# A planner's urgency table, two issuing queues for w_out, and four more weight pieces split on TensorE

## The chip, the cores and the metric

The kernel runs on one core of one Trainium2 chip. The time is device microseconds of that core; lower is better. The kernel before was timed three times: 793.66, 795.12 and 795.73 us, median 795.12.

## The reference, cut to what matters

Block-sparse attention over 4 batches, 8 heads, 768 positions of 64, in blocks of 32 positions; its output is the input of a two-matrix network with the activation h * tanh(softplus(h)).

```python
scores = scale * np.matmul(q, k.transpose(0, 1, 3, 2))
mask = np.abs(blk_i - blk_j) <= 1          # window
mask |= first or last block, as query or as key
for qb in range(n_blocks):                 # and three sampled blocks for each query block
    for kb in sampled_blocks[qb]: mask[...] = True
attn = softmax(where(mask, scores, -1e9)); x = attn @ v      # (3072, 512) after the heads are joined
h = x @ w_in                               # 512 -> 2048
g = h * np.tanh(softplus(h))
out = g @ w_out                            # 2048 -> 512
```

w_in and w_out come as 64-bit floats of 8 MB each; the kernel decodes them itself.

## The kernel before

Every fp32 operand is split into a high and a low fp16 part, so a product is three fp16 matmuls. The work is made of tasks, each with one engine (or a choice of engines), a planned duration, its dependencies and a number `key`. `Plan.emit` writes the instructions of all engines in one pass: for each engine it takes the task that can start first by the planned durations, and among tasks that can start within 0.02 us of each other the one with the smallest ready time plus `key`. The result is a fixed order of instructions on each engine. The engines run these orders in sequence and wait for each other through semaphores.

The work has three kinds.

- **Attention** has 52 jobs, 13 for each batch. A job is one dense query block (the first or the last) or a pair of sparse ones. Its chain runs: scores `s` (L634, PE), maximum `mx` (L681, DVE), exponential `pt` (L700, ACT), transposes `t` (L640, PE), high part `ph` (L723, ACT), low part `pl` (DVE L727; in the first six jobs a matmul with `neg`, L731, and an ACT copy, L736), the product with v into `obank` (L762, PE), a scaling `xs` (L784, DVE), a transpose `tx` (L640), and high and low parts `xh`, `xl` (L809, L818). `xh` and `xl` are rings of three tiles of 256 positions. Tile 0 is complete when job 4 has written its `xl`. From job `WHOLE` on, the keys of a query block are gathered into one piece, so that its scores take half as many matmuls. From job `SPLIT` on, both halves of the product with v are one task.
- **Weights.** w_in comes in 8 pieces of 1 MB (`wr`), w_out in 16 of 0.5 MB (`wor`), issued by ACT (L838). `wor` uses the ring `raw` of six buffers, which holds q, k and v as well. DVE decodes each with three instructions (L846, L849, L852). A bf16 product on PE (`gram`, L334) gives each its scale. A half piece of w_in is then split either on PE (`wd_i`: a matmul with a scaled diagonal, L918, and one with `neg`, L927, with casts on ACT or DVE), or with `wt_i` on ACT, DVE and POOL. `LPE` says how many of four go to PE. w_out is split with `wt_o` (L934 to L941), after all 16 of its pieces have been decoded, since they share one scale (`tp_wo`).
- **MLP.** 12 tiles; `h` (L1016) has 16 tasks of 12 matmuls for a tile, `y` (L1075) 16 tasks of 6. Both keep their order.

MLP tasks have the lowest rank on PE: they go where nothing else can start. Scores are held back by `START` (a planned time for each of the first 14 jobs; a held task still runs when nothing else is ready) and after that by `RES` (L1227, L1242): a job's scores come late until the MLP work done has reached its even share of the total less `RES`. The total is 12 tiles of 16 tasks of 1.31 us and 16 of 1.30 us, or 501 us.

Between 14 and 200 us of planned time, gaps of PE are filled with matmuls that nobody reads (`fill`, L1264), one for each 0.14 us.

Of the kernel before, what the change touches and what calls it, by code (L numbers as in the profile page):

```python
# [29 lines left out]

class Task:
# [9 lines left out]
class Plan:  # L41
# [141 lines left out]
def attn_mish_kernel(ctx: ExitStack, tc: tile.TileContext, qT, kT, v, sampled, blocks, w_in, w_out, out):  # L183
# [117 lines left out]
    NO, NZ = 4 * (D + 2), 240  # L301
    pools = {"w": ctx.enter_context(tc.tile_pool(name="never", bufs=1))}
# [317 lines left out]
    WHOLE = 14  # L620
    SPLIT = 12
# [20 lines left out]
    def attend(job):  # L642
# [188 lines left out]
    def load_w(pool, key, tag, w, a0):  # L831

        if not wide:
            nc.scalar.dma_start(out=a0, in_=w)
# [3 lines left out]
        nc.scalar.dma_start(out=raw.rearrange("p (c f) -> p c f", c=w.shape[1]) if len(w.shape) == 3 else raw, in_=w)  # L838
        tl[key] = raw.rearrange("p (f two) -> p f two", two=2)
# [21 lines left out]
    def load_i(k):  # L861
# [143 lines left out]
    def moe_h(st, fp):  # L1005
        b, t = st
        kh, kq = ("h", b, t, fp), ("hs", b, t, fp // 2)

        def fn(f2):
# [5 lines left out]
            for k, (w, x, cc) in enumerate(prods):  # L1015
                nc.tensor.matmul(h[:, f2].rearrange("p (s q) -> p s q", q=BS), wi[:, fp, cc // 2, w, cc % 2, fs], x[:, :, cc],  # L1016
                                 start=f2 == 0 and k == 0, stop=f2 == 1 and k == len(prods) - 1)
        for f2 in range(2):
            mlp(1.31, lambda f2=f2: fn(f2), r=[*PARTS_I(fp), *xt["x", b, t]], w=[kh, "h in order"],
                new=[("h", kh)] if f2 == 0 else (), use=[("xh", b, t), ("xl", b, t)])  # L1020

        def hs_fn():
            if fp % 2 == 0:
                new(sb, "hs", kq, [P, 4, TT])
            nc.scalar.activation(out=tl[kq][:, 2 * (fp % 2):2 * (fp % 2) + 2], in_=tl[kh], func=AF.Copy,  # L1025
                                 scale=gsc[:, fp:fp + 1])
        add("ACT", 0.72, hs_fn, r=[kh, "gsc"], w=[("hsw", b, t, fp)],
            new=[("hs", kq)] if fp % 2 == 0 else (), use=[kq], key=-4)
        if fp % 2 == 1:
            moe_g(st, fp // 2)  # L1030

    def moe_g(st, k):

        b, t = st
        kq, ku, kg = ("hs", b, t, k), ("us", b, t, k), ("g", b, t, k)
        us, hs, g = (lambda: tl[ku]), (lambda: tl[kq]), (lambda: tl[kg])

        def u_fn():
# [274 lines left out]
```

## Time and profile before

| | |
|---|---|
| time, median of three runs | 795.12 us |
| the profiled execution: time, and its span | 799.4 us, 797.6 us |
| mean granted clock of TensorE | 0.984 |
| PE busy | 747.6 us (94%) |
| ACT, DVE, POOL busy | 542.9, 490.4, 324.2 us |
| moved by DMA | 95.33 MB |

A row of the profile names a line, an engine, an operation, what is written and what is read. "Busy" is the time in which at least one instruction of the group runs. An idle time is put down to whatever ended it. PE is TensorE's matmuls, PEld its weight loads, DVE VectorE, ACT ScalarE, POOL GpSimd and SP SyncE; ACTq and SPq are the instructions that issue DMAs. The span begins with the first instruction and ends with the last; the profiled execution's time is 1.8 us longer than its span.

### The profile page before, as it was taken

To read this page: it belongs to the slowest core of one execution; us is meant where nothing else is said; L and a number is where in the kernel's file an instruction comes from. 1 tells how busy PE (TensorE), PEld (TensorE's weight loads), DVE (VectorE), ACT (ScalarE), POOL (GpSimd) and SP (SyncE) were. 2 spreads that over 40 slices of the span, in tenths; PEclk is the share of its full clock that TensorE was granted. 3 is DMA by queue.
4 is the path that set the end of the run, shared out by engine and by line. 5 is a ranking of instruction groups with operands and counts; after the bars stand their busy time and mean duration, and the time that the engine had idled before them with its cause. 6 is when DMAs were issued, how large, how long until landed. Compare 5 with 4: busy or idle time off the path is not lost.

```text
span 797.6 us, 30868 instructions
## 1 busy us (share of the span) xinstructions
PE 747.6 (94%) x12901; PEld 527.8 (66%) x12901; DVE 490.4 (61%) x897; ACT 542.9 (68%) x881; POOL 324.2 (41%) x397
## 2 busy tenths in 40 slices
PE   6778889798999999999999999999999999999997
PEld 5654668576667777676677766766767767666653
DVE  6868867997776756657746665675676544323220
ACT  3555667769876877787757777878675766465650
POOL 2032246896643544535424543436444231312031
PEclk9999989999999999999999999999999999999999
DMA  8988874304344355246223553343344313000000
GB/s 305 288 242 270 234 193 134 93 21 144 93 143 123 96 162 179 72 110 196 67 82 98 157 154 103 104 150 92 98 125 117 106 40 92 14 14 14 14 14 26
DMA packets 57743, 95.33 MB, mean 120 GB/s; under 512 B 8323, under 2 KB 20612, under 8 KB 57604
## 3 DMA queue, kind: packets, MB, share of 16 engines
q1 hardware_dynamic: 50880, 76.32, 32.6%
q10 hardware_dynamic: 6724, 17.05, 6.7%
q8 instruction: 101, 1.65, 0.9%
q14 instruction: 38, 0.31, 0.1%
HBM read 80.38 MB, written 12.95 MB: 117 GB/s over the span
## 4 chain that ended last, share of the span: by engine, by line
PE 77%; DMA 8%; DVE 7%; ACT 3%; issue 2%; SPq 2%; POOL 1%; POOLq 1%; ACTq 0%; DVEq 0%
PE y L1075 29%; PE h L1016 27%; PE obank L762 6%; PE t L640 6%; PE s L634 5%; DMA wor<-in_moe_w_out_dram 2%; DMA raw_q<-in_q_dram 2%; DMA wr<-in_moe_w_in_dram 2%; DVE wt_o L936 1%; PE tx L640 1%; PE obank L1264 1%; PE wd_i L918 1%; SPq L595 1%; DVE us L1043 1%; DMA raw_k<-in_k_dram 1%
## 5 line engine op out<-in xcount | busy, mean ns | idle before, releaser
L1016 PE MATMUL h<-xh,wi 128*128 128x256 f16 x1536 | 283.5, 274 | 0.0
L1075 PE MATMUL y<-wo,g 128*128 128x512 f16 x1152 | 279.4, 381 | 1.5 <-POOL g L1060 1.5
L1016 PEld LDWEIGHTS <-wi 128*128 128x128 f16 x2304 | 223.0, 98 | 47.3 <-issue 3.0
L1016 PE MATMUL h<-xl,wi 128*128 128x256 f16 x768 | 210.0, 273 | 0.0
L1060 POOL TENSOR_TENSOR g<-hs,g 128x1024 f16<-128x1024 f32 x48 | 109.2, 2276 | 203.7 <-DVE g L1057 137.6
L1075 PEld LDWEIGHTS <-g 128*128 128x128 f16 x1152 | 110.6, 99 | 103.0 <-issue 3.4
L571 POOL COPY kg<-kt 128x256 f16 x255 | 107.8, 454 | 154.3 <-PE s L634 137.3
L1025 ACT ACTIVATE hs<-h,gsc 128x512 f32<-128x512 f32 x96 | 65.5, 684 | 83.0 <-PE h L1016 82.6
L700 ACT ACTIVATE pt<-s,nb,ns 128x256 f32<-128x256 f32 (+1 forms) x208 | 107.2, 580 | 7.5 <-DMA wor<-in_moe_w_out_dram 2.6
L727 DVE SCALAR_TENSOR_TENSOR pl<-t,ph 128x512 f16<-128x512 f32 x99 | 68.0, 687 | 63.4 <-ACT ph L723 63.2
L723 ACT ACTIVATE ph<-t 128x512 f16<-128x512 f32 x112 | 66.7, 596 | 52.7 <-PE t L640 50.0
L1049 DVE SCALAR_TENSOR_TENSOR hs<-us,hs 128x1024 f32<-128x1024 f32 x48 | 60.9, 1268 | 43.6 <-ACT us L1048 43.6
L681 DVE TENSOR_REDUCE mx<-s 128x4 f32<-128x1024 f32 x44 | 53.8, 1222 | 45.5 <-PE s L634 45.5
L1045 POOL TENSOR_TENSOR us<-us 128x1024 f32<-128x1024 f32 x26 | 51.9, 1997 | 60.7 <-DVE us L1043 57.6
L640 PE MATMUL t<-ident,pt 128*128 128x128 f32 x448 | 70.6, 281 | 4.8 <-DVE pl L727 4.4
L640 PEld LDWEIGHTS t<-ident,pt 128*128 128x128 f32 x448 | 53.2, 143 | 18.8 <-DVE pl L727 5.2
L762 PEld LDWEIGHTS <-ph 128*32 128x32 f16 x3584 | 48.0, 94 | 21.7 <-issue 11.8
L1039 ACT ACTIVATE us<-hs,hsc 128x1024 f32<-128x1024 f32 x48 | 55.2, 1151 | 1.2 <-DVE hs L1049 0.5
L1047 ACT ACTIVATE us<-us 128x1024 f32<-128x1024 f32 x48 | 50.7, 1056 | 5.5 <-POOL us L1045 4.7
L762 PE MATMUL obank<-vg,ph 128*32 128x65 f16 (+1 forms) x3200 | 50.7, 196 | 2.1 <-DMA vg<-vd 1.1
L1043 DVE TENSOR_SCALAR us<-us 128x1024 f32<-128x1024 f32 x48 | 39.2, 818 | 19.4 <-ACT us L1039 19.3
L1048 ACT ACTIVATE us<-us 128x1024 f32<-128x1024 f32 x48 | 50.7, 1056 | 0.7
(204 smaller groups left out, 920.8 us busy)
## 6 DMA issues: line engine op xcount, KB each, us to landing
vg<-vd SPq DMA_DIRECT2D x320, 65.0 KB, 2.4
vg<-vd SPq DMA_DIRECT2D x80, 195.0 KB, 3.0
wr<-in_moe_w_in_dram ACTq DMA_DIRECT2D x8, 1024.0 KB, 7.0
wor<-in_moe_w_out_dram ACTq DMA_DIRECT2D x16, 512.0 KB, 6.4
vd<-v SPq DMA_DIRECT2D x12, 520.0 KB, 3.9
vg<-vd SPq DMA_DIRECT2D x12, 520.0 KB, 3.8
raw_k<-in_k_dram SPq DMA_DIRECT2D x12, 512.0 KB, 5.0
raw_q<-in_q_dram SPq DMA_DIRECT2D x12, 512.0 KB, 4.4
```

The lines of the kernel that those rows point to most:

```text
L571: nc.gpsimd.tensor_copy(out=dst, in_=tl["kt", b][:, :, ds(j, BS)])
L640: nc.tensor.matmul(out, src, ident, start=start, stop=stop, is_transpose=True)
L700: ex = lambda o, x, g, w: nc.scalar.activation(out=o, in_=x, func=AF.Exp, bias=nb[:, g, w:w + 1], scale=tl["ns", b, sus[w]["qb"] // TB][:, ...
L723: nc.scalar.activation(out=new(sb, "ph", ("ph", i, j), [P, 2, 2, P], F16), in_=tl["t", i, j], func=AF.Copy, scale=PSC)
L727: nc.vector.scalar_tensor_tensor(out=new(sb, "pl", ("pl", i, j), [P, 2, 2, P], F16), in0=tl["t", i, j], scalar=PSC, in1=tl["ph", i, j], op ...
L762: nc.tensor.matmul(o[cs, w, g, 0:v1 - v0], p[:, k, g, cs], vt[:, k, 2 * c + g, v0:v1], start=j == 0 and g == 0 and k == 0 and n == 0, stop ...
L1016: nc.tensor.matmul(h[:, f2].rearrange("p (s q) -> p s q", q=BS), wi[:, fp, cc // 2, w, cc % 2, fs], x[:, :, cc], start=f2 == 0 and k == 0, ...
L1025: nc.scalar.activation(out=tl[kq][:, 2 * (fp % 2):2 * (fp % 2) + 2], in_=tl[kh], func=AF.Copy, scale=gsc[:, fp:fp + 1])
L1039: nc.scalar.activation(out=new(sb, "us", ku, [P, 4, TT]), in_=hs(), func=AF.Exp, scale=hsc[:, b:b + 1])
L1049: add("DVE", 1.32, lambda: nc.vector.scalar_tensor_tensor(out=hs(), in0=us(), scalar=-0.5, in1=hs(), op0=ALU.add, op1=ALU.mult), r=[ku], w ...
L1060: add("POOL", 2.3, lambda: nc.gpsimd.tensor_tensor(out=g()[:, 1], in0=hs(), in1=g()[:, 0], op=ALU.subtract), r=[kq, ("gh", b, t, k)], w=[kg])
L1075: nc.tensor.matmul(tl[ky], tl["g", b, t, k][:, g, f, q], wo[:, fc, w], start=fc == 0 and n == 0, stop=fc == NFC - 1 and n == 2)
```

## The change

A table adds a number to the key of each task: by its kind, for attention in the first 14 jobs also by the job, and for weights also by the piece. A load of a weight may be issued by ACT or by SP, and the planner chooses. The rest are numbers, and code for half tiles that does not run, because `NHV` is 0 and `HALVES` is empty: `part` is always None.

```diff
+URGE = {"am": -2, "dgi": -11, "endsv": 10, "gh": 6, "gp": -24, "gram": 15, ..., "xw": -3, "ys": -3}
+JOBS = [-11, -1, -1, -13, 3, 4, 2, -13, -38, 3, -19, -28, -1, -34]
+PIECES = [0, 2, -3, -3, -1, -1, 2, 2, -20, -23, -13, -9, -8, -8, -8, -8, -6, -1, -1, 1, -1, 3, 6, 6]
...
+        kind_, i, k = place(w)
+        key += URGE.get(kind_, 0.0) + (JOBS[i] if i is not None else 0.0) + (PIECES[k] if k is not None else 0.0)
...
-    WHOLE = 14
-    SPLIT = 12
+    WHOLE = 12
+    SPLIT = 10
...
+            go = lambda eng: load_w(pools["w"], raw, "wr", src, None, eng)
+            add("ACT", 0.45, lambda: go(nc.scalar), r=after, w=[raw], new=[("wr", raw)], key=-9, lat=2.0,
+                kind=("dma", 3.9), also=[("SP", 0.5, lambda: go(nc.sync), False)] if BOTH else ())
...
+        add("ACT", 0.45, lambda: go(nc.scalar), r=after, w=[raw] + ([] if wide else [("wo", fc)]), new=[("raw", raw)],
+            key=-5, lat=2.0, kind=("dma", 1.95), also=[("SP", 0.5, lambda: go(nc.sync), False)] if BOTH else ())
...
-    LPE = 3
+    LPE = 4
-    AT0, ATV, ATW = -19.0, -13.0, 1.0
+    AT0, ATV, ATW = -19.0, -13.0, -4.0
+    NHV = 0
...
-            PREP = (6, 4, 3) if b else (8, 4, 7)
+            PREP = (6, 4, 3) if b else (7, 3, 6)
-            LOADO, ATO, ATP = [("dec", 5)], -2.0, -22.0
+            LOADO, ATO, ATP = [("dec", 6)], -2.0, -22.0
...
-    RES, START = 145.0, [0, 72, 75, 102, 72, 15, 93, 69, 30, 51, 33, 45, 51, 66]
+    RES, START = 510.0, [0, 99, 19, 112, 114, 119, 80, 0, 11, 132, 80, 43, 18, 0]
```

`PREP` says how many jobs before the end of a batch the next batch's k, v and q are loaded; `LOADO` after which decoded piece of w_in the loads of w_out may begin. A tile of `xl` is still complete when the same jobs have written it.

What this does to the orders is seen at three places. First, on ACT, at the first loads of w_out. Before:

```order
L809 ACTIVATE xh_0_1293<-tx_1653 128x256
L700 ACTIVATE pt_1676<-s_1395,nb_1673,ns_0_270 128x256 x2
L838 DMA wor_1707<-in_moe_w_out_dram 128x1024
L838 DMA wor_1715<-in_moe_w_out_dram 128x1024
L838 DMA wor_1735<-in_moe_w_out_dram 128x1024
L838 DMA wor_1739<-in_moe_w_out_dram 128x1024
L838 DMA wor_1755<-in_moe_w_out_dram 128x1024
L818 ACTIVATE xl_0_1294<-tx_1653 128x256
L723 ACTIVATE ph_0_1768<-t_0_1709 128x512
```

And of the change, at its first loads on ACT:

```order
L951 ACTIVATE wi<-wd_i_0_1998 128x512
L865 DMA wor_2093<-in_moe_w_out_dram 128x1024
L750 ACTIVATE ph_0_2099<-t_0_2039 128x512
L865 DMA wor_2121<-in_moe_w_out_dram 128x1024
L865 DMA wor_2123<-in_moe_w_out_dram 128x1024
L951 ACTIVATE wi<-wd_i_0_2101 128x512
L865 DMA wor_2129<-in_moe_w_out_dram 128x1024
L763 ACTIVATE pl_0_2230<-t_0_2039 128x512
```

Five loads in a row have become four with work between them, and they stand later. ACT issues 8 of the 16 loads, where it issued all.

Second, on SP, which gathers blocks of v (`vg`) for the sparse jobs; the other 8 loads of w_out now stand between the gathers. Before:

```order
L595 DMA vg_112<-vd_60 32x1040
L392 DMA raw_q_2_2331<-in_q_dram 128x4x256
L588 DMA vg_113<-vd_60 96x1040
L595 ISA
L595 DMA vg_113<-vd_60 32x1040
```

Of the change:

```order
L622 DMA vg_112<-vd_60 32x1040
L865 DMA wor_2235<-in_moe_w_out_dram 128x1024
L865 DMA wor_2242<-in_moe_w_out_dram 128x1024
L419 DMA raw_q_2_2325<-in_q_dram 128x4x256
L615 DMA vg_113<-vd_60 96x1040
L622 ISA
L622 DMA vg_113<-vd_60 32x1040
```

Two loads have come ahead of q and of the next gather; two more pairs and two single loads follow at later gathers. The loads of w_in all stay on ACT.

Third, on PE, at job 4's last matmuls on `tx`, after which tile 0 lacks only `xl`. Before:

```order
L815 MATMUL tx_2964<-xh_0_1293,neg 128x128
L815 LDWEIGHTS neg
L815 MATMUL tx_2964<-xh_1_2979,neg 128x128
L918 MATMUL wd_i_0_3039<-wi,dg_i_2967 128x512
L634 LDWEIGHTS q_1_1656
L634 MATMUL s_3060<-kt_228,q_1_1656 32x96
```

Of the change:

```order
L842 MATMUL tx_2943<-xh_1_3090,neg 128x128
L758 LDWEIGHTS neg
L758 MATMUL t_0_2908<-ph_0_3053,neg 128x512
L956 LDWEIGHTS neg
L956 MATMUL wd_i_1_3050<-wi,neg 128x512
L1309 LDWEIGHTS neg
L1309 MATMUL obank<-neg 128x240
```

From the last row on `tx` to the first `h` it was 522 rows on PE, with the scores of two jobs and three pieces of `wd_i`; it is now 115 rows: the two matmuls with `neg`, six fill matmuls, four transposes and one product with v (48 matmuls).

Counted over the whole order of PE, fill matmuls go from 171 to 102: those ahead of the first `h` from 146 to 102, those behind it from 25 to none. The split pieces `wd_i` go from 12 to 16, all ahead of the first `h`. Score matmuls with 96 and 160 columns of keys go down by 48 each, those with 256 up by 48. Ahead of the first `h` now stand the scores of 7 jobs instead of 8, with 96 fewer matmuls, 48 fewer products with v, one fewer each of `t` and `tx` and 8 fewer of w_out's gram.

Behind it, 3 `h` and 3 `y` tasks stood between the scores of one job and of the next for most of the program; now it is 2 and 2 in most places, with stretches of 10 and 10 now and then. At the last job's scores both orders have 149 `h` and 133 `y` tasks, of 192 each, behind them.

More of the change, by code (lines that the diff above doesn't have):

```diff
@@ L1024, in hs_fn @@
                 new(sb, "hs", kq, [P, 4, TT])
-            nc.scalar.activation(out=tl[kq][:, 2 * (fp % 2):2 * (fp % 2) + 2], in_=tl[kh], func=AF.Copy,
+            nc.scalar.activation(out=tl[kq][:, 2 * (fp % 2):2 * (fp % 2) + 2, 0:n], in_=tl[kh][:, :, 0:n], func=AF.Copy,
                                  scale=gsc[:, fp:fp + 1])
-        add("ACT", 0.72, hs_fn, r=[kh, "gsc"], w=[("hsw", b, t, fp)],
+        add("ACT", 0.72 if part is None else 0.45, hs_fn, r=[kh, "gsc"], w=[("hsw", b, t, fp, part)],
@@ L1038, in u_fn @@
         def u_fn():
-            nc.scalar.activation(out=new(sb, "us", ku, [P, 4, TT]), in_=hs(), func=AF.Exp,
-                                 scale=hsc[:, b:b + 1])
-        add("ACT", 1.1, u_fn, r=[("hsw", b, t, 2 * k), ("hsw", b, t, 2 * k + 1), ("hsc", b)], w=[ku],
+            new(sb, "us", ku, [P, 4, TT])
+            nc.scalar.activation(out=us(), in_=hs(), func=AF.Exp, scale=hsc[:, b:b + 1])
+        add("ACT", 1.1 * c, u_fn, r=[("hsw", b, t, f, part) for f in (2 * k, 2 * k + 1)] + [("hsc", b)], w=[ku],
@@ L1047, in moe_g @@
-        add("ACT", 1.07, lambda: nc.scalar.activation(out=us(), in_=us(), func=AF.Ln, bias=1.0), w=[ku])
-        add("ACT", 1.07, lambda: nc.scalar.activation(out=us(), in_=us(), func=AF.Exp, scale=-1.0), w=[ku])
-        add("DVE", 1.32, lambda: nc.vector.scalar_tensor_tensor(
+        add("POOL", 2.0 * c, lambda: nc.gpsimd.tensor_tensor(out=us(), in0=us(), in1=us(), op=ALU.mult), w=[ku],
+            also=[("ACT", 1.07 * c, lambda: nc.scalar.activation(out=us(), in_=us(), func=AF.Square), False)])
@@ L1050, in moe_g @@
+        add("ACT", 1.07 * c, lambda: nc.scalar.activation(out=us(), in_=us(), func=AF.Ln, bias=1.0), w=[ku])
+        add("ACT", 1.07 * c, lambda: nc.scalar.activation(out=us(), in_=us(), func=AF.Exp, scale=-1.0), w=[ku])
+        add("DVE", 1.32 * c, lambda: nc.vector.scalar_tensor_tensor(
             out=hs(), in0=us(), scalar=-0.5, in1=hs(), op0=ALU.add, op1=ALU.mult), r=[ku], w=[kq], port=True)
         def g_fn(eng):
-            new(pools["m"], "g", kg, [P, 2, 4, TT], F16)
+            if not part:
+                new(pools["m"], "g", kg, [P, 2, 4, TT], F16)
@@ L1063, in moe_y @@
+        add("DVE", 0.75 * c, lambda: g_fn("DVE"), port=True, r=[kq, "open"], w=[("gh",) + kp],
+            new=() if part else [("g", kg)], use=[kg], also=[("ACT", 1.07 * c, lambda: g_fn("ACT"), False)])
+        add("POOL", 2.3 * c, lambda: nc.gpsimd.tensor_tensor(out=g(1), in0=hs(), in1=g(0), op=ALU.subtract),
+            r=[kq, ("gh",) + kp], w=[kp], use=[kg])
     def moe_y(st, m, k, last):
@@ L1215, in attn_mish_kernel @@
             scales_b(b)
+    HALVES = order[0:NHV]
     prev = None
```

81 lines of the change are left out of this document (50 added, 31 removed).

## The prediction

> **What bounds the kernel now.** The page first: busy times, the slices in time, and what DMA moved.
>
> ```profile
> PE 747.6 (94%) x12901; PEld 527.8 (66%) x12901; DVE 490.4 (61%) x897; ACT 542.9 (68%) x881; POOL 324.2 (41%) x397
> ...
> PE   6778889798999999999999999999999999999997
> ...
> DMA  8988874304344355246223553343344313000000
> GB/s 305 288 242 270 234 193 134 93 21 144 93 143 123 96 162 179 72 110 196 67 82 98 157 154 103 104 150 92 98 125 117 106 40 92 14 14 14 14 14 26
> ```
>
> PE is the bound, but not in the first five of 40 slices, where DMA is the busiest. So I cut the span into stages: up to the first `h`, up to the first `y`, to 200 us, to 700 us, the end.
>
> ```profile
> core 0: us, PE busy (x) PEld busy (x) DVE busy (x) ACT busy (x) POOL busy (x), PEclk, DMA share, GB/s
> 0.00:109.60 109.60, 82.22 (x1811) 59.89 (x1812) 84.05 (x192) 59.62 (x120) 28.39 (x55) 0.94 0.86 262
> 109.60:147.90 38.30, 34.09 (x728) 28.87 (x725) 30.13 (x53) 28.13 (x52) 24.99 (x28) 0.96 0.43 125
> 147.90:200.00 52.10, 46.31 (x854) 32.82 (x852) 46.09 (x65) 41.84 (x66) 41.22 (x31) 0.97 0.32 97
> 200.00:700.00 500.00, 492.17 (x8929) 348.77 (x8927) 308.63 (x565) 367.58 (x597) 211.95 (x277) 1.00 0.38 110
> 700.00:797.60 97.60, 92.76 (x591) 57.40 (x588) 21.54 (x26) 45.75 (x49) 17.66 (x8) 0.99 0.05 17
> ```
>
> PE's idle time by stage is span less busy: 27.4, 4.2, 5.8, 7.8 and 4.8 us. From 200 us on PE is 98% busy, so what it must do there is time. Ahead of that, part of "busy" is fill that nobody reads. PE's groups by line up to 109.6 us, and the fill behind it:
>
> ```profile
> L1264 PE MATMUL obank<-neg 128*128 128x240 f16 x146 | 19.9, 275 | 5.4 <-DVE xs L784 2.9 <-issue 2.5
> L918 PE MATMUL wd_i<-wi,dg_i 128*128 128x512 f32 x24 | 14.7, 697 | 1.0 <-ACT dg_i L906 0.6 <-ACT wi L922 0.3
> L640 PE MATMUL t<-ident,pt 128*128 128x128 f32 x56 | 9.5, 300 | 0.4 <-ACT pl L736 0.3
> L634 PE MATMUL s<-kg,q 64*32 64x160 f16 x336 | 7.1, 234 | 0.0
> L762 PE MATMUL obank<-vg,ph 128*32 128x65 f16 (+1 forms) x320 | 5.5, 201 | 0.0
> L927 PE MATMUL wd_i<-wi,neg 128*128 128x512 f16 x12 | 4.8, 414 | 0.0
> L334 PE MATMUL gram_wo<-wo 128*128 128x128 bf16 x44 | 4.6, 228 | 0.8 <-DVE wo L852 0.8
> ...
> L1264 PE MATMUL obank<-neg 128*128 128x240 f16 x25 | 4.2, 343 | 1.0 <-DVE xs L784 1.0
> ```
>
> Up to the first `h` PE spends 27.4 us idle and 19.9 us on fill. That 47 us is the room in which an order can gain.
>
> **The change part by part.** *Fill.* 44 fewer matmuls ahead of the first `h`, at 19.9 us / 146, are 6.0 us; the 25 behind it are the 4.2 us of their row. Together -10.2 us, if the gaps that they filled are gone.
>
> *Four more pieces of w_in on PE.* A piece is 14.7 / 12 = 1.23 us (two matmul records) and 4.8 / 12 = 0.40 us: +6.5 us for four. All stand ahead of the first `h`, in place of fill; without that cover they cost 6.5 us. What they replace on ACT, DVE and POOL is off PE's path there.
>
> *Scores.* 96 narrow matmuls at 7.1 us / 336 = 21 ns go, 2.0 us. 48 with 256 columns come. A job with such scores is this row of the timeline:
>
> ```profile
> 219.40 0.85 PE L634 MATMUL s<-kg,q 64*32 64x256 f16 x48
> ```
>
> So -1.2 us, behind 200 us, where PE's work is time. `SPLIT` joins tasks and removes no instruction: nothing, bounded on both sides by the 0.5 us of one wait of PE's product for `pl` below.
>
> The sum so far is -10.2 + 6.5 - 1.2 = **-4.9 us**, with PE's idle time as it was.
>
> *When the first `h` starts.* Tile 0 and `h`, in the timeline of ACT and at line L1016:
>
> ```profile
> 98.57 0.27 ACT L818 ACTIVATE xl<-tx 128x128 f16<-128x128 f32 x1
> ...
> L1016 PE MATMUL h<-xl,wi x768: 270/273/421, 109.9 to 770.2; 128*128 128x256 f16 x192
> ```
>
> The data was there at 98.8 us; `h` came 11 us later, because 522 rows of PE stood between. Now 115 rows stand there: fill 6 x 0.14, a product with v of 0.5 us, four transposes of 0.6 us, two matmuls of 0.4 us, 2.7 us in all; with one wait for a copy on ACT I take 4 us, so the first `h` at 102.8. That isn't 7 us won, since work moved behind it: 96 scores (2.0 us), 48 matmuls with v (0.6), four transposes (0.7), a `tx` (0.2) and 8 of gram (0.8), 4.3 us. PE's busy time ahead of `h` becomes 82.2 - 6.0 + 6.5 - 4.3 = 78.4 us, and the idle time 102.8 - 78.4 = 24.4 us instead of 27.4: **-3.0 us**.
>
> This rests on tile 0 being ready at the same time. Rows for both ends, ACT's waits up to 109.6 us and the loads of w_out:
>
> ```profile
> ACT xl L818 <- DMA wor<-in_moe_w_out_dram: 5.7, 1, 5.7
> ...
> ACT pt L700 <- DMA wor<-in_moe_w_out_dram: 2.6, 1, 2.6
> ...
> ACT dg_i L906 <- DMA wor<-in_moe_w_out_dram: 2.3, 1, 2.3
> ```
>
> These 10.6 us are ACT held at loads that it issues itself, with attention behind it. Half of the loads leave: up to 5.3 us earlier. Against it, the change casts 27 half pieces on ACT ahead of tile 0's last `xl`, where 13 were: 14 x 0.6 us, up to 8.4 us later. DVE's list ahead of job 4's `xs` hardly differs. Between the ends -5.3 and +8.4 I take 0: both come in part.
>
> *The loads themselves.* DMA moved 262 GB/s ahead of the first `h`, at a share of 0.86, and 305 in its best slice; at 305 throughout the stage would be 109.6 x (1 - 262/305) = 15 us shorter, were loading all. I count nothing: SP and ACT both had loads under way already, and the first load of w_out now stands behind more work. The Trainium skill, in "DMA: Bandwidth & Descriptors" under "Issuing engines are not separate DMA queues", says that DMAs of all issuing engines share the same 16 DMA engines, so that spreading them saves only time at the issuer; by that rule the 15 us can't be had and ACT's 10.6 us are all there is, and the share of 0.86 does not contradict it.
>
> *What stands behind SP's loads.* In front of two pairs of gathers and of a load of q there is now a load that must wait for a buffer. Priced below as a rival.
>
> *From the first `h` to 200 us.* Fill goes, but the waits there are for DVE, which splits w_out:
>
> ```profile
> PE t L640 <- DVE pl L727: 4.4, 2, 2.4
> PE tx L640 <- DVE pl L727: 1.8, 1, 1.8
> ...
> PE obank L762 <- DVE pl L727: 0.5, 1, 0.5
> ...
> L936 DVE TENSOR_SCALAR wt_o<-wo,cols x13: 473/617/2350, 133.3 to 177.5; 128x512 f32<-128x512 f32 x13
> ```
>
> DVE still does 12 of these, each up to 2.35 us; the first `y` comes 6 `h` tasks behind w_out's scale instead of 9, with less cover. I leave the idle 10.0 us as they are; ends: all gone (-10.0), or doubled.
>
> *RES.* The MLP is 501 planned us, less than 510: after job 13 nothing holds scores back but buffers. A job then has 2 `h` and 2 `y` beside it, 5.2 us, instead of 3 and 3, 7.8. The work is the same and the end too. I take 0; the ends are -7.8 (all idle time from 200 to 700 us gone) and the rival below.
>
> **Sum**: -4.9 - 3.0 = -7.9 us on a span of 797.6. The profiled execution took 799.4, 4.3 above the median of 795.12; taken off the median it is **787.2 us**.
>
> **The rivals.** *The gaps stay.* Fill counts gaps that the planner foresaw; the idle 27.4 us are gaps that it didn't. If PE waits as long for the chain of attention as before, fill turns into idle time, the split pieces go into it, and only the scores are won: 795.1 - 1.2 = 793.9, no change that can be told. For it: DVE is busy 84 of 109.6 us ahead of `h`, and its list there is no shorter. Against it: the 522 rows become 115.
>
> *Denser attention starves PE* (slower). From 200 to 700 us, ACT's groups of attention, its `hs` (one for two `h` tasks), and DVE's `xs` (one a job):
>
> ```profile
> L700 ACT ACTIVATE pt<-s,nb,ns 128x256 f32<-128x256 f32 (+1 forms) x156 | 80.0, 580 | 3.3 <-PE t L640 2.5
> L723 ACT ACTIVATE ph<-t 128x512 f16<-128x512 f32 x84 | 50.0, 596 | 42.7 <-PE t L640 42.5
> L1025 ACT ACTIVATE hs<-h,gsc 128x512 f32<-128x512 f32 x68 | 46.6, 685 | 54.4 <-PE h L1016 54.0
> ...
> L809 ACT ACTIVATE xh<-tx 128x256 f16<-128x256 f32 (+1 forms) x47 | 15.5, 342 | 8.1 <-PE tx L640 5.5 <-PE h L1016 2.6
> ...
> L690 ACT ACTIVATE nb<-mx,ns 128x4 f32<-128x4 f32 (+1 forms) x45 | 12.4, 288 | 8.7 <-DVE mx L681 5.8 <-DVE mx L679 2.3
> ...
> L784 DVE TENSOR_TENSOR xs<-obank,r 128x256 f32<-128x256 f32 (+1 forms) x41 | 16.6, 405 | 1.5
> ```
>
> 41 jobs take 492.2 / 41 = 12.0 us of PE each, with 136 / 41 = 3.3 `h` and as many `y`, 8.6 us; 3.4 are attention. ACT works 367.6 / 41 = 9.0 us a job, of them 157.9 / 41 = 3.9 for attention. With 2 and 2 a job has 8.6 us of PE and 3.9 + 5.1 x 2/3.3 = 7.0 of ACT: 81% instead of 74%. PE lost 7.8 us there, 0.2 us a job. If chains on ACT and DVE then come late by 0.5 us a job, that is 20.5 less 7.8: 787.2 + 12.7 = 799.9. It is slower by over 0.3% from +10.3 us on. Against it: 81% leaves room, and attention ahead of need gives MLP work to fill with.
>
> *SP's loads hold up gathers.* 8 loads at ACT's 10.6 / 16 = 0.66 us are 5.3 us, if each delays a job's product with v: 792.5, still faster.
>
> *The clock falls with less fill.* The granted clock in two windows:
>
> ```profile
> 100.00:120.00 20.00, 16.45 (x349) 12.26 (x337) 12.94 (x29) 13.35 (x26) 8.61 (x14) 0.85 0.70 189
> ...
> 150.00:165.00 15.00, 12.26 (x215) 9.20 (x200) 13.77 (x27) 11.48 (x16) 11.78 (x8) 0.89 0.23 73
> ```
>
> It fell to 0.85 with fill beside it. At 0.85 instead of 0.94 the 64 us of work ahead of `h` become 64 x (0.94/0.85 - 1) = 6.8 us longer: 794.0. The Trainium skill, in "TensorE: Matmul & The Clock Gate" under "What's actually happening", says that an idle window of about 3.4 us halves the clock until PE has been busy for such a window; by that rule 69 fewer fill matmuls are a risk wherever a gap stays, and the trace agrees in so far as 0.85 and 0.89 stand where PE idles most.
>
> *More is won*: 10.0 us behind the first `h` half gone, and 4 at 200 to 700: 778.
>
> **How the numbers follow.** Chances: the forecast 0.52, SP's loads 0.08, more won 0.08, gaps stay 0.13, the clock 0.04, denser attention 0.15. Faster by over 0.3% (2.4 us, about what a measurement of this kernel can tell from no change) is 0.52 + 0.08 + 0.08 = 0.68; within it 0.13 + 0.04 = 0.17; slower 0.15. The low end is "more won" at 778; the high end takes in "the gaps stay" and stops short of denser attention's 799.9: 797.
>
> **What would show it.** The first `h` at 103 us; ACT's waits at loads of w_out about 5 us, and SP's below 5; no fill behind the first `h`; idle time from 109.6 to 200 us near 10; PE idle from 200 to 700 us near 8. The forecast is wrong if tile 0's `xl` lands after 105 us, if idle time takes fill's place, or if PE's waits for DVE and ACT behind 200 us exceed 18 us.

## The result, and the profile after

| | before | change |
|---|---|---|
| median | 795.91 us (792.01 to 798.85, 10 runs) | 791.11 us (789.48 to 792.17, 10 runs) |
| ratio, 95% interval | | 0.995 [0.993, 0.997] |
| profiled execution, its span | 799.4, 797.6 us | 790.27, 788.5 us |
| first `h`, first `y` | 109.8, 148.0 us | 108.1, 147.0 us |

The change is faster by 4.0 us against the median that the forecast started from, and by 4.8 us against before's runs beside it. The forecast was 7.9: the direction and the range held, the size did not.

The page of the change, with the rows that were shown of before:

```profile
PE 746.7 (95%) x12796; PEld 523.2 (66%) x12796; DVE 494.4 (63%) x897; ACT 549.4 (70%) x890; POOL 304.0 (39%) x386
...
PE   6778798979999999999999999999999999999997
...
DMA  8876875123444365144246613442433112000000
GB/s 309 286 230 191 267 223 169 49 82 123 144 125 133 102 186 192 53 153 144 60 131 178 207 51 96 136 117 80 130 103 104 51 49 84 15 14 14 14 14 27
```

PE is busy 0.9 us less than before; 4.9 less were forecast, so most of what this profile won is idle time. The same windows as in the prediction (up to before's first `h`, up to its first `y`, to 200 us, to 700 us, the end):

```profile
core 0: us, PE busy (x) PEld busy (x) DVE busy (x) ACT busy (x) POOL busy (x), PEclk, DMA share, GB/s
0.00:109.60 109.60, 83.97 (x1633) 56.92 (x1634) 79.94 (x181) 61.55 (x125) 25.02 (x52) 0.91 0.78 251
109.60:147.90 38.30, 36.09 (x881) 30.14 (x880) 33.22 (x66) 31.26 (x55) 21.62 (x21) 0.96 0.59 170
147.90:200.00 52.10, 47.30 (x722) 33.19 (x721) 46.85 (x60) 41.22 (x65) 44.16 (x36) 0.97 0.28 86
200.00:700.00 500.00, 495.68 (x9037) 351.44 (x9036) 314.35 (x569) 374.34 (x605) 195.55 (x270) 1.00 0.37 110
700.00:788.50 88.50, 83.62 (x529) 51.48 (x527) 20.05 (x24) 41.00 (x44) 17.66 (x8) 0.99 0.05 19
```

Idle time (width less PE busy) is 25.6, 2.2, 4.8, 4.3 and 4.9 us where it was 27.4, 4.2, 5.8, 7.8 and 4.8. From the first `h` to the end it is 680.4 us instead of 687.8, so 7.4 of the 9.1 us between the two spans lie behind the first `h`, where the forecast had put the smaller part (0.9 of 7.9: `h` was to come 7.0 us earlier). PE's groups that the sum spoke of, and tile 0's last `xl` on ACT with line L1049 (`h`, L1016 before):

```profile
L661 PE MATMUL s<-kg,q 64*32 64x256 f16 (+1 forms) x2112 | 39.5, 263 | 0.8 <-issue 0.8
L947 PE MATMUL wd_i<-wi,dg_i 128*128 128x512 f32 x32 | 19.9, 725 | 1.7 <-ACT wi L951 1.6
L661 PE MATMUL s<-kt,q 64*32 64x96 f16 (+2 forms) x864 | 19.6, 270 | 0.0
L1309 PE MATMUL obank<-neg 128*128 128x240 f16 x102 | 16.3, 314 | 2.9 <-DVE xs L811 2.6 <-issue 0.3
L956 PE MATMUL wd_i<-wi,neg 128*128 128x512 f16 x16 | 6.7, 418 | 5.3 <-ACT wi L951 4.3 <-DVE wi L953 0.9
```

```profile
107.48 0.47 ACT L845 ACTIVATE xl<-tx 128x128 f16<-128x128 f32 x2
...
L1049 PE MATMUL h_None<-xl,wi x768: 270/273/421, 108.2 to 761.0; 128*128 128x256 f16 x192
```

The count of fill went as forecast, but the 102 that remain take 0.16 us each instead of 0.14, so 7.8 us of fill are gone in this profile and not 10.2. The pieces of w_in cost a little more, 7.1 us (26.6 instead of 19.5) for 6.5. Tile 0 was complete at 107.95 us instead of 98.8, and `h` followed within 0.2 us: the 11 us between them are gone, but because tile 0 comes 9.1 us later. The prediction had named this as a sign that it is wrong: tile 0's `xl` after 105 us. ACT's waits at loads of w_out (10.6 us) are gone too; one wait has come at a load of w_in (ACT issues it at 50.02 us and then casts `wi`), and PE waits for this cast, 3.9 us at once:

```profile
ACT wi L951 <- DMA vg<-vd: 4.8, 1, 4.8
...
PE wd_i L956 <- ACT wi L951: 4.3, 2, 3.9
```

### The profile page after: what moved, and what is told of

Its sections match the earlier page's. It is cut to its first block, busy times and chain, and to the rows that moved or that the text cites. A ratio compares the mean times of both kernels' runs of the same rounds, so it can differ in the third digit from the quotient of the medians.

```text
span 788.5 us, 30661 instructions
## 1 busy us (share of the span) xinstructions
PE 746.7 (95%) x12796; PEld 523.2 (66%) x12796; DVE 494.4 (63%) x897; ACT 549.4 (70%) x890; POOL 304.0 (39%) x386
## 4 chain that ended last, share of the span: by engine, by line
PE 78%; DVE 9%; DMA 7%; issue 2%; ACT 2%; SPq 1%; POOLq 0%; ACTq 0%; DVEq 0%
PE h_None L1049 29%; PE y L1114 28%; PE t L667 6%; PE obank L789 6%; PE s L661 4%; DMA vg<-vd 3%; PE wd_i L947 1%; DMA wr<-in_moe_w_in_dram 1%; PE tx L667 1%; DVE v L491 1%; DMA raw_q<-in_q_dram 1%; DMA wor<-in_moe_w_out_dram 1%; DVE g L1096 1%; DMA raw_k<-in_k_dram 1%; DVE wo L969 1%
## 5 line engine op out<-in xcount | busy, mean ns | idle before, releaser
L1049 PE MATMUL h_None<-xh,wi 128*128 128x256 f16 x1536 | 283.9, 274 | 0.6 <-issue 0.6
L1114 PE MATMUL y<-wo,g 128*128 128x512 f16 x1152 | 277.6, 379 | 2.8 <-POOL wo L970 1.1
L1049 PEld LDWEIGHTS <-wi 128*128 128x128 f16 x2304 | 224.2, 98 | 48.7 <-issue 3.0
L1049 PE MATMUL h_None<-xl,wi 128*128 128x256 f16 x768 | 209.9, 273 | 0.0
L1099 POOL TENSOR_TENSOR g<-hs_None,g 128x1024 f16<-128x1024 f32 x48 | 106.3, 2215 | 220.3 <-DVE g L1096 143.9
L1114 PEld LDWEIGHTS <-g 128*128 128x128 f16 x1152 | 110.8, 98 | 104.0 <-issue 4.4
L1060 ACT ACTIVATE hs_None<-h_None,gsc 128x512 f32<-128x512 f32 x96 | 65.7, 685 | 72.5 <-PE h_None L1049 71.4
L1087 DVE SCALAR_TENSOR_TENSOR hs_None<-us_None,hs_None 128x1024 f32<-128x1024 f32 x48 | 63.8, 1330 | 46.6 <-ACT us_None L1086 45.5
L1083 POOL TENSOR_TENSOR us_None<-us_None 128x1024 f32<-128x1024 f32 x18 | 35.8, 1990 | 65.9 <-DVE us_None L1081 63.5
L1078 ACT ACTIVATE us_None<-hs_None,hsc 128x1024 f32<-128x1024 f32 x48 | 55.2, 1151 | 0.8
L1085 ACT ACTIVATE us_None<-us_None 128x1024 f32<-128x1024 f32 x48 | 50.7, 1056 | 3.2 <-POOL us_None L1083 2.3
L789 PE MATMUL obank<-vg,pl 128*32 128x65 f16 x1600 | 48.2, 194 | 3.9 <-DVE pl L754 3.4
L1081 DVE TENSOR_SCALAR us_None<-us_None 128x1024 f32<-128x1024 f32 x48 | 37.3, 777 | 23.2 <-ACT us_None L1078 23.1
```

The costliest lines, as they stand in the source:

```text
L789: nc.tensor.matmul(o[cs, w, g, 0:v1 - v0], p[:, k, g, cs], vt[:, k, 2 * c + g, v0:v1], start=j == 0 and g == 0 and k == 0 and n == 0, stop ...
L1049: nc.tensor.matmul(h[:, f2, 0:n].rearrange("p (s q) -> p s q", q=BS), wi[:, fp, cc // 2, w, cc % 2, fs], x[:, s0:s0 + sn, cc], start=f2 == ...
L1078: nc.scalar.activation(out=us(), in_=hs(), func=AF.Exp, scale=hsc[:, b:b + 1])
L1087: add("DVE", 1.32 * c, lambda: nc.vector.scalar_tensor_tensor(out=hs(), in0=us(), scalar=-0.5, in1=hs(), op0=ALU.add, op1=ALU.mult), r=[ku ...
L1099: add("POOL", 2.3 * c, lambda: nc.gpsimd.tensor_tensor(out=g(1), in0=hs(), in1=g(0), op=ALU.subtract), r=[kq, ("gh",) + kp], w=[kp], use=[kg])
L1114: nc.tensor.matmul(tl[ky], tl["g", b, t, k][:, g, f, q], wo[:, fc, w], start=fc == 0 and n == 0, stop=fc == NFC - 1 and n == 2)
```

## The experiments

Each kernel is compared with runs of before made beside it.

**Before again.** No edit.

> The kernel before once more, for a second profile. Theory A (the profiled execution of before was a slow one: 799.4 us against a median of 795.9): the span is 793 to 796 us, PE idles 45 to 48 us instead of 50, and the missing idle time is ahead of 200 us. Theory B (the profile was typical and medians differ for another reason): the span is again 797 to 798 us with 50 us of idle time in the same places.

797.34 us (792.11 to 804.36, 12 runs). The profiled execution has a span of 793.0, with the first `h` at 108.7 and idle time of 26.5 us up to 109.6 and 6.4 from 200 to 700. Before scatters over 12 us, and the profile that the prediction was made from was one of its long ones, as the first theory had it.

**RES, each way.** `RES = 145.0` in the change, and `RES = 510.0` in before.

> The change with RES back at 145; the order of PE up to job 9 is the same as the change's. Theory A (letting attention run ahead won PE's idle time between 200 and 700 us, 7.8 against 4.3 us): the time goes up by 3 to 4 us to about 794.5 and PE idles 7 to 8 us between 200 and 700. Theory B (the difference there is run-to-run variation or comes from the order of the first 200 us): 791 us within 1, idle time there 4 to 5 us.

> The kernel before with RES 510 alone; same order up to job 9 as before. Theory A (RES won the idle time behind 200 us): faster by 3 to 4 us, about 792. Theory B (it did not): 796 within 1. The rival of the prediction (denser attention starves PE): slower, over 798, with PE waiting for DVE and ACT behind 200 us.

The change with the old RES: 791.91 us, ratio 0.993 [0.990, 0.9961], idle 4.4 us from 200 to 700. Before with the new: 798.45, ratio 1.0022 [0.9992, 1.0053], idle 8.0. Neither way can RES be told from no change. 798.45 us lies just over the 798 of the rival of denser attention, but the waits that it needs aren't there: from 200 to 700 us PE waits 1.7 us for ACT and DVE with RES 510 in before (0.9 with 145), and 1.2 us in the change (2.8 with 145).

**Before without fill.** `FILL = 0.0, 0.0`.

> The kernel before without its 171 fill matmuls, the order otherwise the same (FILL = 0, 0). Theory A (fill stands in gaps that exist anyway; removing it turns its 24 us of busy time into idle time): 796 us within 1.5, PE busy 724, granted clock up to 110 us lower than 0.94. Theory B (fill is in the way of work that is ready earlier than planned): faster, 790 or less. Theory C (fill keeps the clock up, and the clock ahead of the first h is time): slower by 3 us or more.

800.03 us, ratio 1.0027 [0.9993, 1.0062]. Its windows up to its first `h`:

```profile
0.00:107.90 107.90, 70.42 (x1666) 46.87 (x1667) 83.36 (x193) 59.05 (x120) 27.86 (x56) 0.87 0.86 266
```

19.9 us of fill are gone there, and PE is busy only 12 us less: without fill it was busy 82.2 - 19.9 = 62.3 us, and now the same work takes 70.4. The clock is 0.87 instead of 0.94, which by itself would give 62.3 x (0.94/0.87 - 1) = 5.0 of these 8 us, by estimate. Over the whole span PE is busy 11 us less, not the 24 of the first theory. The first `h` comes at 107.9, within 2 us of both profiles of before: 12 us less of work on PE ahead of `h` did not bring `h` forward by more than that.

**One part of the change undone**: no table (`key += 0.0`), all loads on ACT (`BOTH = False`), `LPE = 3`, and the old `START`.

> The change without its table (every task keeps its old key); both queues, four pieces of w_in split on PE, START, RES, WHOLE and SPLIT of the change stay. Theory A (the table's order carries the gain): ratio to the kernel before 0.999 to 1.004, about 796 us, and PE's idle time behind the first h back to about 20 us where the change has 16. Theory B (the table only shuffles work that has slack, the numbers carry it): ratio 0.992 to 0.997, 789.5 to 793 us, idle behind the first h as in the change. The first h tells what pushed tile 0: if it stays at 107 to 110 us, the table isn't what made tile 0 nine microseconds later than before.

> The change with all loads of weights on ACT again. Theory A (the second queue frees ACT): ACT's waits at loads of w_out come back with about 10 us up to the first h, tile 0's xl comes 5 us or more later than 108 us, 794 to 797 us. Theory B (DMA is the limit and only the place of the waiting moves): first h within 2 us of the change's 108.1, 790 to 792.5 us, ratio 0.992 to 0.997. The 4.8 us in which ACT was held at a load of w_in until a gather of SP's had landed stay in B, and go in neither by themselves.

> The change with three of four pieces of w_in split on PE as before (12 instead of 16). Theory A (the casts on ACT and the matmuls of four more pieces push tile 0 back): xl of tile 0 ready at 100 to 104 us, first h at 101 to 105, PE busy ahead of it 4 us or more lower, 786 to 789 us. Theory B (those pieces stood in idle time and tile 0 waits for DMA and DVE): first h at 107 to 110, 790 to 793 us; with the four pieces on DVE and POOL again it may be 1 to 2 us later than the change.

> The change with the planned start times of the first 14 jobs' scores as before. Theory A (START orders attention and weights ahead of the first h and so sets tile 0): 500 more rows of PE and 46 more fill matmuls up to the first h, which then comes at 112 us or later, 794 to 797 us. Theory B (rows ahead of the first h fill time that is there anyway): first h at 107 to 110, 790 to 793 us, ratio 0.992 to 0.997.

| | us (12 runs) | ratio | first `h` | first `y` |
|---|---|---|---|---|
| no table | 802.59 | 1.0072 [1.0038, 1.0106] | 112.6 | 165.9 |
| all loads on ACT | 801.77 | 1.0062 [1.0029, 1.0095] | 116.2 | 156.6 |
| LPE 3 | 792.73 | 0.9951 [0.9918, 0.9984] | 106.8 | 140.8 |
| old START | 802.67 | 1.0077 [1.0045, 1.011] | 120.8 | 170.5 |

Without any one of the table, the second queue and START the rest is some 10 us slower than the change, and slower than before (by 0.6 to 0.8%). Each is further off than the first theory of its expectation had it, and the second queue not by the way named there: with all loads on ACT, its waits at loads of w_out are one of 3.6 us, not 10. What the three share is that `h` and above all `y` start later; that this is the cause is not shown. Line L1114 (`y`) of the change, without the table, and with the old START:

```profile
L1114 PE MATMUL y<-wo,g x1152: 376/379/390, 147.0 to 784.1; 128*128 128x512 f16 x192
```

```profile
L1114 PE MATMUL y<-wo,g x1152: 376/379/390, 165.9 to 794.9; 128*128 128x512 f16 x192
```

```profile
L1114 PE MATMUL y<-wo,g x1152: 376/379/390, 170.5 to 795.6; 128*128 128x512 f16 x192
```

LPE moves the total by less than its interval: what four more pieces cost on PE comes out of idle time and fill, which are 4.9 us more with 3. With 3 instead of 4, tile 0's last `xl` on ACT and the first `h`:

```profile
103.41 0.46 ACT L845 ACTIVATE xl<-tx 128x128 f16<-128x128 f32 x2
...
L1049 PE MATMUL h_None<-xl,wi x768: 270/273/421, 107.0 to 762.3; 128*128 128x256 f16 x192
```

Tile 0 is complete at 103.87, 4.1 us earlier than in the change, as the first theory said; but `h` comes only 1.3 us earlier, just ahead of the second theory's 107, and the total lies within the second's 790 to 793.

**WHOLE and SPLIT undone, denser fill, the three alone, no fill.** `WHOLE, SPLIT = 14, 12`; a fill matmul for each 0.10 us instead of 0.14; table, second queue and START with every other number as before; `FILL = 0.0, 0.0`.

> The change with the old WHOLE and SPLIT (scores of two more jobs narrow, products with v in two tasks for two more jobs); the order up to the first h is the change's to the row. Theory A (the prediction's: 96 narrow score matmuls against 48 wide ones, 1.2 us, and SPLIT nothing): 792 to 794 us, PE's idle time from 200 to 700 us within 1.5 us of the change's 4.3. Theory B (the fewer, joined tasks are what took the waits put down to issue out of 200 to 700 us): idle there back at 6.4 to 8 us, 794 to 797 us. First h at 107.5 to 109.5 us in both.

> The change with one fill matmul for each 0.10 us of a planned gap instead of 0.14: 148 ahead of the first h instead of 102, 7 behind; nothing else moves. Theory A (the clock of 0.91 ahead of the first h, 0.94 to 0.95 before, costs about 2 us; more fill gives it back): clock ahead of h 0.93 to 0.95, first h 1 to 3 us earlier, 788.5 to 790.5 us. Theory B (tile 0's chain on DVE, ACT and DMA sets the first h, and neither fill nor clock is in it): first h at 107 to 110, 790.5 to 793. Theory C (the prediction's way of counting, 46 more fill matmuls are time): +6 us, 797.

> The table, the second queue and START alone: LPE 3, WHOLE 14, SPLIT 12, RES 145, PREP, LOADO and ATW as before. Each of the three was worth about 10 us with all the rest in place. Theory A (they are worth it by themselves): 789 to 793 us, ratio 0.990 to 0.997. Theory B (the table's numbers hold for one schedule only, and small edits elsewhere spoil them): the first h at another place, fill 195 instead of 102, idle time and fill up to 200 us of 62 us or more where the change has 49, and 796 to 803 us.

> The change without any fill (its 102 matmuls, 16.3 us of PE's busy time, all ahead of the first h); the order is the change's otherwise. Theory A (fill ahead of the first h is no time in itself, it only holds the clock): PE's busy time falls by less than 12 us, clock ahead of h 0.85 to 0.88, first h at 107 to 111, 791 to 794.5 us. Theory B (fill is time that the first h waits for): the first h 5 us or more earlier, 785 to 788 us.

| | us | ratio | first `h` | clock ahead of it | idle 200 to 700 |
|---|---|---|---|---|---|
| WHOLE 14, SPLIT 12 | 795.43 | 1.0015 [0.9989, 1.0041] | 108.4 | 0.94 | 8.0 |
| denser fill | 793.49 | 0.9988 [0.996, 1.0016] | 106.2 | 0.94 | 8.0 |
| three alone | 815.74 | 1.0267 [1.0232, 1.0302] | 98.7 | 0.95 | 14.2 |
| no fill | 786.54 | 0.9911 [0.9879, 0.9943] | 108.1 | 0.89 | 3.0 |

The three parts alone bring the first `h` at 98.7 and the first `y` at 119.0 us, 20 us later: the earliest of all, and the slowest kernel, slower than both theories of its expectation (796 to 803 us in the second). From 120 to 700 us PE waits there 13.0 us for attention's exponentials and high and low parts and for `g`, where the change waits 5.1. That fits the second theory: an early `h` is worth nothing if too little attention is ready to go with it, and the table's numbers fit one schedule.

This run also narrows down what holds tile 0. With table, second queue and START, and the rest as before, tile 0 is complete at 98.2 us, as early as before's 98.8. So the 9.1 us come with the rest, on top of these three: 4.1 us of them with LPE, as above. RES, and WHOLE with SPLIT, leave the order of PE, ACT, DVE and POOL up to the first `h` as it is, and without them `h` came at 109.0 and 108.4. PREP, LOADO and ATW remain for the other 5 us; none of them was run alone.

The first of the four met its second theory to the number (8.0 us idle, 795.43), which the last six runs take back: the change itself has 8.2 and 8.6 at other places. Denser fill did what its first theory said of the clock (0.94) and of `h` (1.9 us earlier), and the total went the other way. No fill left the first `h` where it was, as its first theory said, and the time came out in the range of its second. Denser fill and no fill have the change's order of work behind the first `h` (but for 7 fill matmuls in the denser one), and yet the idle time there differs. The waits of PE from 200 to 700 us, in the change and with denser fill:

```profile
PE obank L789 <- DMA vg<-vd: 1.1, 2, 0.6
PE s L661 <- issue: 0.8, 2, 0.5
...
PE obank L789 <- issue: 0.6, 2, 0.5
PE h_None L1049 <- issue: 0.6, 2, 0.4
```

```profile
PE h_None L1049 <- issue: 3.3, 2, 2.0
PE s L661 <- issue: 2.0, 2, 1.2
```

Waits put down to issue (they end with nothing that the profile shows) sum to 2.0 us behind the first `h` in the change, 7.1 with denser fill, and 6.4 and 6.1 in before's two profiles. 53 fill matmuls moved them, most of them 100 us ahead.

**Where the blocks of PE's program end.** The theory here is that PE's instructions come in blocks of a fixed size, and that PE waits for issue where a block ends. The next six runs put 32, 64 or 96 tiny matmuls at the very start of PE's program, where it waits for k; each also has a weight load, so all that follows stands 64, 128 or 192 instructions further. Each such shift, and none, is called a place below: the order of work is the same, and the block ends fall elsewhere in it.

```diff
+    for _ in range(64):
+        nc.tensor.matmul(obank[0:32, NO:NO + 8], neg[0:32, 0, 0:32], neg[0:32, 0, 0:8], start=True, stop=True)
     plan.emit(pace, fill)
```

> The change with 32 tiny matmuls (32x32 weights, 8 columns, nobody reads them) at the very start of PE's program, where PE waits for k until 4.7 us: every later PE instruction stands 64 places further, nothing else moves. Theory A (waits put down to issue come at the ends of blocks of 256 PE instructions): they stand at other matmuls than in the change, still a multiple of 127 matmuls apart, their sum behind the first h anywhere from 1 to 7 us, and the time moves with it, 789 to 796 us. Theory B (they belong to the work around them): same matmuls, sum 1.5 to 2.5 us, time 790 to 792.5 us.

> As the run before with 64 tiny matmuls, a shift of 128 PE instructions. Theory A: other places than at shifts of 0 and 64, sum of waits for issue behind the first h between 1 and 7 us, 789 to 796 us. Theory B: 1.5 to 2.5 us at the change's places, 790 to 792.5 us.

> As the run before with 96 tiny matmuls, a shift of 192 PE instructions. Theory A: other places again, 1 to 7 us, 789 to 796 us; over the four shifts the change's median of medians lies 3 us or less under before's. Theory B: 1.5 to 2.5 us at the change's places, 790 to 792.5 us at each shift.

> Before with the same 64 tiny matmuls at its start. Theory A (blocks): waits for issue behind the first h at other matmuls than in both profiles of before, sum anywhere from 1 to 7 us instead of 6.1 to 6.4, 791 to 799 us. Theory B (the order of before makes them): 5.5 to 7 us at the same places, 795 to 798 us.

> Before with 32 tiny matmuls at its start. The change's four shifts gave 791.1, 788.3, 799.2 and 793.3 us, mean 793.0; before stands at 796 (shift 0) and 798.1 (64 matmuls). Theory A (the order is worth about 4 us, the shift adds to either sign): 794 to 800 us, and the mean of before's four 3 to 5 us above 793.0. Theory B (the gain is only the place of the blocks): this run or the next at 788 to 792 us, and the means within 1.5 us.

> Before with 96 tiny matmuls at its start. Theory A: 794 to 800 us, as the run before. Theory B: 788 to 792 us here or there. In both, waits put down to issue behind the first h between 1 and 7 us, at matmuls other than in before's own profiles.

| tiny matmuls | 0 | 32 | 64 | 96 | mean |
|---|---|---|---|---|---|
| change, us | 791.11 | 788.28 | 799.23 | 793.27 | 793.0 |
| ratio | 0.995 | 0.9909 | 1.0043 | 0.9971 | 0.9968 |
| before, us | 795.91 | 799.81 | 798.09 | 797.73 | 797.9 |
| ratio | 1 | 1.0041 | 1.0039 | 1.0027 | 1.0027 |
| waits for issue behind the first `h`: change, us | 2.0 | 4.7 | 9.1 | 6.2 | 5.5 |
| the same, before, us | 6.4 | 6.2 | 5.0 | 2.9 | 5.1 |

(The intervals of the ratios are 0.0025 to 0.0032 to either side, 0.002 for the change itself. The waits are of the one profiled execution each; that of 64 in the change was, at 793.01 us, the shortest of its 12 runs.)

The same order of work gives anything from 788.3 to 799.2 us, which is the first theory of the shifts, and wider at both ends than its 789 to 796; before's four stay within 4 us, and the means lie 4.9 us apart, more than the 3 expected of the third run and within the 3 to 5 of the fifth. Place by place the change is ahead by 4.8, 11.5 and 4.5 us and at 64 behind by 1.1, which can't be told from none. The sums of waits don't put the medians in order: with 32 the change waits more than with none and is faster, and before waits least with 96 and is slower than with none. So that the place moves the time is shown; that it does so through these waits alone is not.

The waits stand at fixed counts of instructions. Before, the timeline at its first four waits for issue, and windows that end there, whose third number is the count of matmuls:

```profile
36.01 0.21 PE L762 MATMUL obank<-v,ph 128*32 128x64 f16 x2 [0.45 <-issue]
41.39 0.89 PE L1264 MATMUL obank<-neg 128*128 128x240 f16 x7 [2.52 <-issue]
51.18 0.23 PE L634 MATMUL s<-kt,q 64*32 64x96 f16 x6 [1.60 <-issue]
57.92 0.56 PE L334 MATMUL gram_wi<-wi 128*128 128x128 bf16 x7 [1.42 <-issue]
```

```profile
0.00:36.01 36.01, 24.18 (x350) 19.76 (x351) 27.30 (x65) 15.90 (x22) 5.84 (x19) 0.95 0.87 297
0.00:41.39 41.39, 27.04 (x479) 22.18 (x479) 31.93 (x75) 18.36 (x28) 7.05 (x22) 0.96 0.87 290
0.00:51.18 51.18, 35.23 (x604) 28.33 (x605) 38.24 (x91) 24.90 (x42) 8.17 (x23) 0.93 0.88 287
0.00:57.92 57.92, 39.31 (x732) 31.34 (x733) 43.26 (x99) 29.06 (x51) 13.21 (x28) 0.94 0.88 284
```

Before with 64 tiny matmuls ahead, the same two views:

```profile
41.25 0.31 PE L634 MATMUL s<-kg,q 64*32 64x160 f16 x2 [4.42 <-issue]
58.24 0.30 PE L762 MATMUL obank<-vg,ph 128*32 128x65 f16 x7 [4.63 <-issue]
75.23 0.25 PE L634 MATMUL s<-kg,q 64*32 64x160 f16 x5 [0.53 <-issue]
```

```profile
0.00:41.25 41.25, 27.61 (x478) 22.54 (x478) 27.77 (x68) 15.90 (x22) 5.84 (x19) 0.95 0.87 288
0.00:58.24 58.24, 39.98 (x732) 31.61 (x733) 39.15 (x92) 27.44 (x48) 13.22 (x28) 0.91 0.86 275
0.00:75.23 75.23, 55.11 (x988) 41.15 (x988) 52.41 (x121) 34.96 (x63) 15.09 (x29) 0.89 0.85 274
```

The counts are 350, 479, 604, 732 and 478, 732, 988: steps of 128 or 256 but for one or two missing records. The wait at 478 hits a fill matmul in one program and a score in the other; the change waits at 350 and 478 too, and with 64 tiny matmuls at 478. 128 matmuls with their weight loads are 256 instructions. The page of the profile lists a queue that moves instructions, here of the change:

```profile
q8 instruction: 100, 1.64, 0.8%
```

100 packets of 16.4 KB. Their number goes with PE's program: it has 2 x 12,796 = 25,592 instructions in the change, 100 times 256, and 25,802 in before, whose page has 101 packets. Taking these packets' times from the trace, each wait for issue ends shortly after one has landed; for the four of before (us from the span's start):

```
wait ends   its length   packet starts   packet has landed
36.01       0.45         33.45           34.54
41.39       2.52         38.78           40.14
51.18       1.60         48.42           49.60
57.92       1.42         55.56           56.74
```

So it is for all 36 such waits in the profiles of before, of the change, and of both with 64 tiny matmuls: they end 1.2 to 1.7 us after a packet's landing. PE has run through a block and waits for the next. The Trainium skill, in "Runtime: NRT & Kernel Launch" under "Instruction fetch mechanics", has blocks of 256 instructions of 16 KiB, which the trace bears out, and calls the cost of crossing from one to the next mostly hidden. Here no wait for issue is seen at about nine of ten ends, and one of up to 4.63 us at the others.

## Why the forecast was right in direction and wrong in size

Over the four places the profiles of both orders can be compared term by term (means of four, worked out from the windows and groups of each profile; "the rest" is what is left of the span's difference):

| us | before | change | difference | forecast |
|---|---|---|---|---|
| fill ahead of the first `h` | 22.1 | 16.0 | -6.1 | -6.0 |
| fill behind it | 3.8 | 0 | -3.8 | -4.2 |
| `wd_i`, both kinds | 18.3 | 26.1 | +7.8 | +6.5 |
| scores, all together | 50.1 | 50.4 | +0.4 | -1.2 |
| PE idle ahead of the first `h` | 26.0 | 25.1 | -0.9 | -3.0 |
| PE idle from it to 200 us | 9.8 | 7.0 | -2.8 | 0 |
| PE idle from 200 to 700 us | 7.3 | 6.5 | -0.8 | 0 |
| the rest of PE's work | | | -0.5 | 0 |
| span | 797.3 | 790.6 | -6.7 | -7.9 |

These are single executions: their spans differ by 6.7 us, where the medians differ by 4.9, and the change's with 64 tiny matmuls was 6 us under its median.

*Right: fill and the pieces.* The counts came out, and over the four places so did fill's 9.9 us. The pieces cost 1.3 us more than forecast. RES at 0 held, by two runs. Splitting four more pieces on PE showed no cost in the total (LPE 3 changes it by less than its interval).

*Wrong: the price of a narrow score.* 7.1 us / 336 = 21 ns was taken from one row, but the scores on `kg` and on `kt` alternate and their busy times overlap. All scores of before up to 109.6 us, of before over the whole span, and of the change (us, PE busy and the count of matmuls, then clock and DMA):

```profile
0.00:109.60 109.60, 8.91 (x720) 0.94 0.86 262
...
0.00:797.60 797.60, 49.97 (x3024) 0.98 0.40 120
...
0.00:788.50 788.50, 50.25 (x2976) 0.98 0.40 121
```

720 take 8.91 us, 12 ns each, so 96 are 1.2 us and not 2.0, and the forecast of -1.2 should have been -0.3. Measured is +0.3 here and +0.4 over the four places: nothing was won.

*Wrong, and the step that failed: "this rests on tile 0 being ready at the same time".* The prediction took 0 between -5.3 and +8.4 us. It was +9.1 in the profiled execution, just beyond the late end, so the first `h` came at 108.1 and not at 102.8, and the -3.0 of idle time was -1.8. Over the four places tile 0 is complete at 107.5 instead of 100.8, +6.8 us and within the ends; `h` comes at 107.7 instead of 110.5, and the -3.0 was -0.9. 4.1 us of the 9.1 went with the extra pieces, by LPE 3. ACT's 10.6 us of waits at loads of w_out went whole, and tile 0 came later all the same. ACT's 4.8 us at a load of w_in are not the rest: with 32 and with 64 tiny matmuls the change has no such wait, and that `xl` begins at 108.5 and 105.6. By the run of the three parts alone, PREP, LOADO and ATW are left to hold tile 0 for the other 5 us, by themselves or together with the table; which of them does is open.

*Wrong in kind: that stage's PE time as the thing that sets `h`.* Two kernels without fill kept `h` within 2 us of their twins, denser fill brought it forward, and the three parts alone had it earliest and ended last. It fits these runs, and is not shown, that what is saved ahead of `h` counts only as far as attention and w_out's scale, which gates `y`, come earlier too: the three kernels whose first `y` came after 156 us ended above 801, but so did the three parts alone, with the earliest `y`.

*Too small: idle time from the first `h` to 200 us.* I left it at 10.0, with "all gone" as an end; some 30% of it went, 2.8 us.

*Missing from the sum: the place of the program against its blocks.* The change's own profile shows idle time from 200 to 700 us 3.5 us lower. The forecast had 0 there; the rival "more is won", given a chance of 0.08, had 4 us there and 5 us ahead of 200. But over the four places the gain from 200 to 700 us is 0.8 us, and the waits for issue behind the first `h` are 5.5 us against 5.1: the order is not seen to lower them. That the one profile came near the rival there is luck of the place. By place the change's medians run from 2.8 us under to 8.1 us over its own. Neither the forecast nor its range had a term for that. The change happens to stand at a better place than the mean of its four, before at its best.

*The base.* The sum was made against a span of 797.6; the second profile of before, of the same program, has 793.0. Those 4.6 us are as much as the change won. The profile of the change lies 9.1 us under the first of them, more than was forecast, and 4.5 under the second.

*The clock.* The prediction says that 0.85 and 0.89 stand where PE idles most. Its own table of stages speaks against it: up to the first `h` PE idles a larger share, 27.4 of 109.6 us, at 0.94. The lower clock with less fill was seen (0.91 instead of 0.94 ahead of `h`), but what it is worth in the total the fill runs leave open.

What remains of the gain as a property of the order is 0.9968 against 1.0027, 0.6% or 4.7 us. With four places each, of which the change's differ by a standard deviation of 4.6 us, that has a standard error of some 2.5 us. So a gain of the order is likely and not beyond doubt, and the forecast's -7.9 lies outside what was measured at the one place and not clearly outside what the order is worth.

*Open.* The undone parts and the fill runs also move the blocks, and their ratios carry that. The table, the queue and START undone, and the three alone, lie above all four of the change's places, but the first three by only 2.5 to 3.5 us above the highest (799.23), so how much of their 10 us is the parts' own is open; what WHOLE, denser fill and no fill show in the total does not, and was not run at other places. No fill, at 786.54 us, and the change with 32 tiny matmuls, at 788.28, are faster than both kernels. Why no fill wins 4.6 us with 2.6 us of waits for issue behind `h` against the change's 2.0 isn't explained: 1.2 us of it lie between first `h` and first `y`, at a clock of 1.00 instead of 0.96, the rest behind.

## What to carry to other kernels

Before a profile's stage is turned into a forecast, profile the same kernel twice: what differs between the two is the floor of the working. In a kernel whose bound engine runs tens of thousands of small instructions, shift its program by a fraction of a block with a few instructions that cost next to nothing (32 tiny matmuls took 1.0 us here, during a wait), and compare both versions over several shifts before a per cent is given to an edit. And where a table of urgencies has been fitted, its parts have no worth of their own: undone one at a time each seemed to be worth 10 us, and the three alone lost 20. Where two rows of short instructions alternate, take their price from both rows together.

## What the runs showed of the hardware that was not expected

- PE waits at the ends of blocks of 256 instructions for the next packet of 16.4 KB: 9.9 to 17.3 us in all in the profiles of before's four places, 5.1 to 11.3 in those of the change, single waits up to 4.63 us. The four of over 4 us fell where DMA's share was 0.90 or more in the 4.5 to 5.3 us before they ended; with a share of 0.36 there was still one of 2.14 us (before again, at 393.8).
- Moving PE's program by 64 or 128 instructions, with 1.0 to 1.9 us of tiny matmuls in a wait, moved the change's median by -2.8 and +8.1 us.
- Without fill the granted clock ahead of `h` fell from 0.94 to 0.87 in before and from 0.91 to 0.89 in the change; in before the same work then took about 8 us longer (62.3 to 70.4 us) and `h` did not come later.
- ACT, as an issuer, was held for 4.8 us at its own load of w_in, and the profile puts the end of the wait down to the landing of a gather that SP had issued (7.6 us in the change with RES 145, none with 32 or 64 tiny matmuls). Why the load waits for it is not shown.
